# Window attention over row and column pairs: column heads staged in 128-channel tiles, one output product a block, stores of two blocks, and nine tiles off ScalarE in nine column pairs

## The chip, the cores and the metric

One core of one Trainium2 chip. The time is the device time of one execution in microseconds (us); shown are the runs of the kernel before and one profiled execution. TensorE is PE in the profile, VectorE is DVE, ScalarE is ACT, GpSimd is POOL, and SyncE, which issues most DMAs, is SP.

## What is computed

A picture `x` of 224 x 224 tokens with 96 channels gets queries, keys and values by one product with `wqkv`. The first 48 channels attend within horizontal stripes of 8 rows, the other 48 within vertical stripes of 8 columns; each stripe has 1792 tokens. The two results are joined channel by channel and multiplied with `wo`.

```python
qkv = jnp.einsum('bhwc,cd->bhwd', x, wqkv)
q, k, v = (qkv[..., :C], qkv[..., C:2 * C], qkv[..., 2 * C:])
scale = C2 ** (-0.5)                      # C = 96, C2 = 48, sw = 8
qh = q[..., :C2].reshape(B * nh, sw * W, C2)          # 28 horizontal stripes
ah = _softmax(jnp.einsum('bqc,bkc->bqk', qh, kh) * scale, axis=-1)
oh = jnp.einsum('bqk,bkc->bqc', ah, vh).reshape(B, H, W, C2)
...                                                   # ov: the same for 28 vertical stripes
o = jnp.pad(oh, ((0, 0), (0, 0), (0, 0), (0, C2))) + jnp.pad(ov, ((0, 0), (0, 0), (0, 0), (C2, 0)))
return jnp.einsum("bhwc,cd->bhwd", o, wo)
```

All arrays are bfloat16. The inputs are small, so the softmax is taken without a maximum; a mean key is taken off every key instead.

## The kernel before

**Stages.** Two stripes are worked at a time: 14 stages over row pairs (`P` from 0 to 13), then 14 over column pairs (`P` from 14 to 27). Stripe `w` of the pair lies in partitions `64 * w` and up. A stage has four chunks of queries (512, 512, 512 and 256 columns) against 14 blocks of 128 keys; a tile is one key block (two, in the last chunk) against one chunk for both stripes, 128 x 1024 scores. That makes 49 tiles a stage.

**A tile on ScalarE (kind A).** PE writes the scores into one of two pairs of PSUM banks (L689, four quarter products), ScalarE writes the exponentials of all 1024 columns into a buffer `PT` (L859), and PE multiplies them with V (L715), adding into one of four other banks, the ring.

**A tile off ScalarE (kinds P and R).** The exponential is worked out from a polynomial and a square. PE writes the scores into two banks of the ring (L702). DVE makes `qb` from their low halves (L943). For kind P, GpSimd squares `qb` into `PT` (L959), applies a scale and offset (L960), and squares again (L956); for kind R, DVE does a second pass (L945) and GpSimd only the one square (L956). Then PE writes the scores a second time (L702 again), and DVE joins them with `PT` (L948). Either DVE pass can be one instruction over both banks or two over one each. `KINDS` gives the tiles off ScalarE by chunk and `KIND_OF` the choice for each stage: eight in stage 0, nine (five P, four R) in stages 1 to 13, eight (five P, three R) in the columns.

**Order.** The work of PE is written out by hand in `ORDER`, one letter a step: q is a tile for ScalarE, v its product with V, 1 and 3 the first pass of a tile off ScalarE (one bank at a time, or both at once), 2 and 4 its second pass, k a step of preparing the next stage (K, the mean key, Q, V), g a part of the output product, f a part of the last pair's output. The mode A (q, 1 to 4, f) and the mode B (v, k, g) use the array in different shapes. `Sched.commit` turns each step into instructions with waits on semaphores; while it walks the letters it keeps estimated times (`tm`, `D_*`, `XR1`, `TURN`) to decide the order on DVE, GpSimd and the queues. These figures never run on the chip; they only decide who stands in front of whom. Each engine works strictly in its own order.

**Heads.** After a chunk, DVE copies its sums out (`emit_ot`, L876). A DMA transpose on SP's queue (`turn_ot`, L423) turns them to tokens in partitions, and GpSimd multiplies with the reciprocals of the sums (`emit_norm`, L920). For a row pair the result is `ohn`, and `keep_oh` copies it by DMA into the place of all column pairs in `cat` (96 channels a token, row heads in the first 48). For a column pair it goes into the last 48 channels of `cat`. `turn_cat` (L445) then transposes this pair's 28 blocks of 128 tokens x 96 channels with a DMA, 128 x 128 at a time: 28 x 96 / 128 = 21 tiles, in two parts of 12 and 9. So the blocks don't begin at the start of a tile, but at one of four offsets.

**Output.** `out_fills` (L623) does five blocks a step. A block's 96 channels lie in one transposed tile or in two, so a block takes one product or two, each in halves of 64 tokens (L637), against six shifted copies of `wo` with zeros around (`wo6`). DVE copies the sums into `cat` (L642), and a store of each block, 128 tokens of 192 bytes, follows on SP's queue (`emit_evict`, L897). The last pair is different: its row-head half is multiplied early, and `fin_fills` (L585) adds the column half at the end, block by block (L602, L609, L614), with stores on SP's, ScalarE's and GpSimd's queues.

**Start.** The first row pair is loaded directly by four DMAs of 168 KB, two on SP's queue and two on ScalarE's, then `wqkv` on SP's (L315 to L320); PE transposes it (L737), with DVE and ScalarE copying out (L749, L753). GpSimd sets constants meanwhile (L300 to L362).

Of the kernel before, what the change touches and what calls it, by code (L numbers as in the profile page):

```python
# [5 lines left out]
BF16 = mybir.dt.bfloat16  # L6
FP16 = mybir.dt.float16
FP32 = mybir.dt.float32
# [12 lines left out]
KINDS = ["PPR PPR PP ", "PPR PRR PPR ", "PPR PPR PR "]  # L21
# [11 lines left out]
D_ST, D_SW, D_TAIL = 0.64, 1.3, 0.70  # L33
XR1, XR2, TURN = 19.5, 43.0, 4.5
D_H, D_F, D_SQ, D_AF = 0.604, 1.137, 1.9, 1.03
# [4 lines left out]
NTWICE = 11  # L40


KIND_OF = [0, 1, 1, 1, 1, 1, 1, 1, 1, 1, 1, 1, 1, 1, 2, 2, 2, 2, 2, 2, 2, 2, 2, 2, 2, 2, 2, 2]
ORDER = [
    "kkkqkq3qkq3qkkqkq1qkqq1q3qvkqv2qvkqv2qvqkkvqv1qkvqvkqvv2qvqv1qvvvqvkq2vqvkqkq1qkvvq2qvv2qvvq1vqkvqvvq1vqv2qvkvqvkvq",
    "1vqvvqvq2vvq3qvvvqvv3qqvqvvqkkkq2qvqvkvqv2qkvqv2qkvvvq1qvvvvqvqvv1qvvq2vq2qvkqvvq1vqvkq2vqv2qvvq1qvvqvkqvvkqkvqvkq2vvq2qvv3",
    "qvvqv1qvvq1vqvvqvvqv1qkq1qvvvqvq2qvkkqvqvk2qvvq3qvkqvkvq4qkqv1qvvq4qvkq2vqv1qvq4vqkq2vqv1qvvqvvqv2q1qvvqvkkqq1vkv",
    "qv2qvqv1qvvvqvvqv1qq1vvqvvqvvvq4qvkvq1vqvvqvq2vqv1qvv4qkqvv1qvqvkq2vqkvvq2vkqvkq3vqkqvvvqv1qvq4vqkq3vqkvq4vqvkvq4vqkvq2vk",
    "qvvq1vqvvvvqq2vvvqvvvq2vqvq14qvqkqv3qvkvqvvqvkqv1qkqvvq1vqvkq2vqvkq2qvvvq1qv1qkqvvvqkqvvkq2qvv3qkvqv3qvvqv4qvkqv4qkqvv1",
    "qvqvvvq2vqq1vvqvv1qvvqvqv2qq4vqvkq1vqvvvqvq1vqkvkqkvvq2kqv3qkvqv4qvvqkq1vqvvvqkqvv4qvqkv2qvvq2vqv1qvq4vqvvqkvkvq1qkvvq2v",  # L50
# [123 lines left out]
def bass_standalone__window_attn_cswin__vision_kernel(  # L174
# [28 lines left out]
    with es:  # L203
# [1153 lines left out]
```

## Time and profile before

| | us |
|---|---|
| runs of the kernel before (three) | 1061.93, 1062.24, 1062.27 |
| profiled execution, its own time | 1062.68 |
| span of that execution in the trace | 1060.9 |
| first exponential begins (L859) | 9.57 |
| GpSimd's first square begins (L959) | 12.81 |
| last exponential ends | 1055.98 |
| granted TensorE clock, mean | 0.999 |

In rows of costly groups stand the line, engine, operation and names, then the count, the busy time, the mean duration in ns, and the idle time of that engine just before these instructions with what ended it. A row of the windows has the stretch and its length, then the busy time of PE, PEld (weight loads), DVE, ACT and POOL with counts, the granted clock and the DMA share. A row of a timeline has the start, the length, the engine and line, and how many such instructions follow one another. Instructions of one engine can overlap, so a mean duration can be longer than the pace.

### The profile page before, as it was taken

Reading aid. Unit: us, or ns where it says so; the run is one execution under the profiler, and the core shown is the slowest. Engines: PE = TensorE matmul, PEld = TensorE weight load, DVE = VectorE, ACT = ScalarE, POOL = GpSimd, SP = SyncE. Lnnn points to the kernel's source line nnn. Section 1 sums busy time; section 2 is a strip of 40 time slices with the busy share of each in tenths; the row PEclk is TensorE's granted clock in tenths of the full one; section 3 lists DMA queues with packets and bytes.
Section 4 is the critical chain, followed back from the end, with each engine's and each line's share of the span. In section 5 each row is a group of like instructions: output and inputs, shape, how many; then the busy total and the mean of one; then the engine's idle time right before and its main releaser. Section 6 shows DMA issues by size and latency. Waiting matters only on the chain.

```text
span 1060.9 us, 33547 instructions
## 1 busy us (share of the span) xinstructions
PE 1033.4 (97%) x13812; PEld 393.5 (37%) x13812; DVE 998.2 (94%) x1720; ACT 1049.3 (99%) x1146; POOL 935.5 (88%) x617
## 2 busy tenths in 40 slices
PE   9999999999999999999999999999999999999998
PEld 4333333333333333333334433333343443344433
DVE  8999999999999999999999999999999999999988
ACT  8999999999999999999999999999999999999998
POOL 7999999999988989999999778888888878979784
PEclk9999999999999999999999999999999999999999
DMA  9987648754963874322115334423332342332342
GB/s 182 160 153 112 100 80 145 112 96 84 144 96 56 139 108 69 38 56 58 40 20 99 76 54 76 88 38 77 80 69 52 81 83 49 79 79 40 64 65 44
DMA packets 376217, 88.58 MB, mean 83 GB/s; under 512 B 366944, under 2 KB 373376, under 8 KB 376064
## 3 DMA queue, kind: packets, MB, share of 16 engines
q1 hardware_dynamic: 374816, 85.85, 46.8%
q8 instruction: 108, 1.77, 0.7%
q10 hardware_dynamic: 1120, 0.49, 0.2%
q14 instruction: 45, 0.37, 0.1%
q0 software_dynamic: 128, 0.10, 0.0%
HBM read 28.36 MB, written 28.21 MB: 53 GB/s over the span
## 4 chain that ended last, share of the span: by engine, by line
PE 54%; ACT 28%; DVE 7%; issue 6%; POOL 4%; DMA 0%; ACTq 0%; POOLq 0%; DVEq 0%
ACT PT L859 28%; PE ps L715 20%; PE ps L689 20%; PE ps L702 7%; PE ps L521 3%; DVE qb L943 2%; DVE PT L948 2%; PE ps L637 2%; POOL PT L959 2%; PE ps L566 1%; POOL PT L956 1%; POOL PT L960 1%; DVE PT L945 1%; DVE KT_sb L526 1%; POOL cat L920 0%
## 5 line engine op out<-in xcount | busy, mean ns | idle before, releaser
L859 ACT ACTIVATE PT<-ps 128x1024 bf16<-128x1024 f32 x1135 | 1044.8, 1087 | 2.8 <-PE ps L689 1.8
L689 PE MATMUL ps<-QT_sb,KT_sb 49*64 49x512 bf16 (+1 forms) x5368 | 465.3, 363 | 17.6 <-ACT PT L859 10.5
L956 POOL TENSOR_TENSOR PT<-PT 128x1024 f16<-128x1024 f16 x237 | 445.1, 1892 | 41.1 <-DVE PT L945 24.1
L715 PE MATMUL ps<-PT,V_sb 128*49 128x512 bf16 (+1 forms) x3136 | 464.7, 362 | 0.3
L948 DVE SCALAR_TENSOR_TENSOR PT<-ps,PT 128x512 uint16<-128x512 f32 (+1 forms) x398 | 302.0, 787 | 20.8 <-PE ps L702 13.5
L943 DVE TENSOR_SCALAR qb<-ps 128x512 f16<-128x512 int16 (+1 forms) x404 | 302.3, 778 | 20.3 <-PE ps L702 15.8
L959 POOL TENSOR_TENSOR PT<-qb 128x1024 f16<-128x1024 f16 x141 | 266.1, 1892 | 54.8 <-DVE qb L943 24.9
L689 PEld LDWEIGHTS ps<-QT_sb,KT_sb 49*64 49x64 bf16 x5368 | 136.4, 103 | 305.8 <-ACT PT L859 280.9
L715 PEld LDWEIGHTS ps<-PT,V_sb 128*49 128x49 bf16 x3136 | 134.8, 103 | 211.1 <-issue 181.4
L702 PE MATMUL ps<-QT_sb,KT_sb 53*64 53x512 bf16 (+1 forms) x1896 | 189.4, 389 | 4.0 <-DVE PT L948 0.7
L960 POOL TENSOR_SCALAR PT<-PT 128x1024 f16<-128x1024 f16 x141 | 147.1, 1043 | 12.0
L945 DVE SCALAR_TENSOR_TENSOR PT<-ps,qb 128x512 f16<-128x512 int16 (+1 forms) x166 | 122.5, 766 | 0.5
L702 PEld LDWEIGHTS ps<-QT_sb,KT_sb 53*64 53x64 bf16 (+1 forms) x1896 | 53.8, 104 | 71.2 <-DVE PT L948 21.7
L876 DVE CAST OT_sb<-ps 113x512 bf16<-113x512 f32 x112 | 69.1, 617 | 3.0 <-PE ps L715 2.7
L535 DVE CAST QT_sb<-ps 128x512 bf16<-128x512 f32 (+1 forms) x111 | 67.2, 616 | 2.5 <-PE ps L521 1.7
L526 DVE TENSOR_SCALAR_CACHE_REDUCE KT_sb<-ps 128x512 bf16<-128x512 f32 x108 | 65.4, 616 | 1.3 <-PE ps L521 0.6
L642 DVE CAST cat<-ps 128x480 bf16<-128x480 f32 x84 | 51.5, 617 | 5.1 <-PE ps L637 4.5
L573 DVE CAST V_sb<-ps 128x480 bf16<-128x480 f32 (+1 forms) x84 | 51.7, 620 | 1.5 <-PE ps L566 1.2
L521 PE MATMUL ps<-xT_sb,w_sb 97*64 97x512 bf16 (+1 forms) x224 | 40.7, 364 | 0.0
L521 PE MATMUL ps<-xT_sb,wq_sb 97*64 97x512 bf16 x224 | 40.5, 366 | 0.1
L637 PE MATMUL ps<-wo,oc_all 128*64 128x96 bf16 x1176 | 39.9, 208 | 0.0
L566 PEld LDWEIGHTS ps<-w_sb,xT_sb 96*64 96x64 bf16 x1568 | 33.1, 112 | 17.7 <-issue 7.4
(64 smaller groups left out, 254.7 us busy)
## 6 DMA issues: line engine op xcount, KB each, us to landing
xT_sb<-xt_dram SPq DMA_DIRECT2D x28, 336.0 KB, 4.0
out_dram<-cat SPq DMA_DIRECT2D x382, 24.0 KB, 1.9
xp_dram<-in_x_dram SPq DMA_DIRECT2D x26, 336.0 KB
oc_all<-xp_dram SPq DMA_DIRECT2D x26, 336.0 KB, 4.4
xt_dram<-xT_sb SPq DMA_DIRECT2D x26, 336.0 KB, 6.4
cat<-ohn SPq DMA_DIRECT2D x52, 84.0 KB, 3.2
xt_dram<-xT_sb SPq DMA_DIRECT2D x4, 168.0 KB, 5.3
OT_tr<-OT_sb SPq DMA_TRANSPOSE x40, 3.4
```

Of the source, the lines that this page charges most:

```text
L521: ins = e.matmul(bk[64 * w:64 * w + 64, 0:qs], lhsT=lw, rhs=xT_sb[b][0:C + 1, w, q0:q0 + qs], start=True, stop=True)
L526: return e.tensor_scalar(KT_sb[b][:, q0:q0 + qs], bk[:, 0:qs], alpha, None, ALU.mult, ALU.add, accum_out=ksum[b][:, c:c + 1])
L689: ins = e.matmul(bank(SETS[s] + w)[64 * kh:64 * kh + 64, i * t["qs"]:(i + 1) * t["qs"]], lhsT=KT_sb[b][64 * w:64 * w + CA, kt * 128 + 64 * ...
L702: ins = e.matmul(bank(bp[w])[64 * kh:64 * kh + 64, 0:512], lhsT=KT_sb[b][64 * w:64 * w + nr, kt * 128 + 64 * kh:kt * 128 + 64 * kh + 64], ...
L715: ins = e.matmul(bank(pb)[64 * w:64 * w + CA, 0:t["qs"]], lhsT=V_sb[b][:, w, kt, :], rhs=PT[slot][:, ca:ca + t["qs"]], start=st and i == 0 ...
L859: S.commit("act", 0.0, D_ACT, None, lambda e, s=s, slot=slot: e.activation(PT[slot][:], ps[:, 512 * SETS[s]:512 * SETS[s] + 1024], ACTF.Ex ...
L943: fn, reads, writes = lambda e: e.tensor_scalar(q, l, m, a, ALU.mult, ALU.add), bk, qk
L945: fn, reads, writes = lambda e: e.scalar_tensor_tensor(y.bitcast(FP16), l, -RA * 2.0 ** 16, q, ALU.add, ALU.mult), bk + qk, ptk
L948: fn, reads, writes = lambda e: e.scalar_tensor_tensor(y.bitcast(U16), f, 128.0, y.bitcast(FP16), ALU.mult, ALU.add), bk + ptk, ptk
L956: square = ("pool", D_SQ, lambda e: e.tensor_tensor(y, y, y, ALU.mult), yk + ["pser"], yk)
L959: return [("pool", D_SQ, lambda e: e.tensor_tensor(y, q, q, ALU.mult), qk, yk), ("pool", D_AF, lambda e: e.tensor_scalar(y, y, -(QS * (RB ...
L960: ("pool", D_AF, lambda e: e.tensor_scalar(y, y, -(QS * (RB + RA) / 2) ** 2, 1.0, ALU.add, ALU.mult), yk + ["pser"], yk),
```

## The change

- **Nine pairs.** `KINDS` gets a fourth entry with nine tiles off ScalarE (six P, three R). Stages 15, 16, 17, 19, 20, 21, 23, 24 and 25 use it; 14, 18, 22, 26 and 27 stay at eight.
- **Order.** 23 of the 28 lines of `ORDER` are new; the lines of the middle of the row half are kept. A capital K or G stands for two steps of the same sort that fill two neighbouring banks and are copied out by one DVE instruction (`do_fill2`, `emit_both`); there is one of each.
- **Staging.** `cat` is replaced by `oh_all` (the kept row heads of all pairs, 48 channels a token), two staging tiles `stg` (one pair each, 28 blocks of 128 channels, the last 32 of them zero), and three output tiles `og`. For each column pair a new DMA on SP's queue, `rows_in`, copies the row heads from `oh_all` into `stg`, in runs of 96 bytes; `emit_norm` writes the column heads beside them. For the last pair and the first, both copies stand at the changeover, ahead of the last pair's transposes.
- **Products.** `turn_cat` transposes 28 tiles of 128 x 128 instead of 21. A block is one tile, so it takes one product (in two halves) against one copy of `wo`.
- **Stores.** A half of the array now takes a whole key block, and the products take every second token of it, so that two neighbouring tokens end up in one partition. A store covers two blocks: 128 partitions of 384 bytes. A column pair has 14 stores, and so has the last.
- **Start.** The first half of the load is cut in four DMAs of 84 KB, the second in two of 168 KB; `wqkv` goes over GpSimd's queue. The memsets of `stg` (448 and 1792 words of 32 bits a partition) join GpSimd's constants at the start, and the ones for `cat` and `wo6` (672 and 288 words) go from the later ones.

```diff
-KINDS = ["PPR PPR PP ", "PPR PRR PPR ", "PPR PPR PR "]
+KINDS = ["PPR PPR PP ", "PPR PRR PPR ", "PPR PPR PR ", "PPR PPR PPR "]
...
-KIND_OF = [0, 1, 1, 1, 1, 1, 1, 1, 1, 1, 1, 1, 1, 1, 2, 2, 2, 2, 2, 2, 2, 2, 2, 2, 2, 2, 2, 2]
+KIND_OF = [0, 1, 1, 1, 1, 1, 1, 1, 1, 1, 1, 1, 1, 1, 2, 3, 3, 3, 2, 3, 3, 3, 2, 3, 3, 3, 2, 2]
...
-    "v1qvvqvvqvvq2gqvvvq1vqgvqgvq2vqvvq2vvq3qvqgvq2vqvq1vqfvvqvvfqvfqvfqvv2qgqvvq1q2qvgqvvq1gqvqvvqv2qvvfqvfqvvfqvfq2vqvvqvqvvffqfvvvvfvff",
+    "q2qvvv1qvvq2vqv2qvvvq1qvvvqvvq1qvvq4vgqvvq1vqv2qvvq3vqgvvqvvqvq2vfqvvfqvvfqv1qvvq4vqgvq4vqgvqvv1qfqvvvqvvfqv4qvqg2qvfqfvvfqvvqvgqvvgvffvvvvfvff",
...
-        cat = sb("cat", [128, NPH, NPH, 2, C], BF16)
+        oh_all = sb("oh_all", [128, NPH, NPH, 2, C2], BF16)
+        stg = [sb(f"stg{i}", [128, NKT, 2, 128], BF16) for i in range(2)]
+        og = [sb(f"og{i}", [128, NKT // 2, 2, 2, C], BF16) for i in range(3)]
...
+        for h2, q in ((0, "sp"), (1, "actq")):
+            for w in range(2):
+                dma(q, [], [("x", w, 0, h2)], x0_sb[:, w, h2 * FQ:(h2 + 1) * FQ, :],
+                    x_lead[w][:, h2 * FQ * C:(h2 + 1) * FQ * C], f"x{w}0{h2}", land=3.1 + 0.4 * w + 0.2 * h2)
+        for w in range(2):
+            dma("sp", [], [("x", w, 1, 0), ("x", w, 1, 1)], x0_sb[:, w, FTH:2 * FTH, :],
+                x_lead[w][:, FTH * C:2 * FTH * C], f"x{w}10", land=4.7 + 0.3 * w)
...
+        dma("gq", [], ["wst"], wst[:, :], wqkv, "w0", land=4.6)
...
-            pool_now([("cat", NPH - 1)], lambda e: e.memset(cat[:, NPH - 1, :, :, C2:C].rearrange("p m w c -> p (m w) c").bitcast(FP32), 0.0), 0.7)
-            pool_now(["wo6z"], lambda e: e.memset(wo6[:].rearrange("p v c -> p (v c)").bitcast(FP32), 0.0), 0.3)
+        pool_now([("stgz", 0)], lambda e: e.memset(stg[0][:, :, :, C:].rearrange("p m w c -> p (m w) c").bitcast(FP32), 0.0), 0.5)
+        pool_now([("stgz", 1)], lambda e: e.memset(stg[1][:, :, :, :].rearrange("p m w c -> p (m w c)").bitcast(FP32), 0.0), 1.8)
...
+        def rows_in(P):
+            b = P % 2
+            dma("sp", ["oh", ("stgz", b)], [("sr", b)], stg[b][:, :, :, 0:C2].rearrange("p m w c -> p (m w) c"),
+                oh_all[:, P - NPH, :, :, :].rearrange("p m w c -> p (m w) c"), f"ri{b}")
...
-            turn(f"oc{b}{z}", ["oh", ("cat", a), ("ov", a, z)], [("ocT", b, z), ("catd", a, z)] + x_old,
-                 oc_T[b][:, k0 * 2 * C // 128:k1 * 2 * C // 128, :], flat[:, k0 * 2 * C:k1 * 2 * C])
+            turn(f"oc{b}{z}", [("sr", b), ("sc", b, z), ("stgz", b)], [("ocT", b, z)] + x_old,
+                 oc_T[b][:, 2 * k0:2 * k1, :], stg[b][:, k0:k1, :, :].rearrange("p m w c -> p (m w c)"))
...
-        dst_all = out[0].rearrange("(kt hh) (j dw) c -> j kt hh dw c", hh=16, dw=8)
+        dst_all = out[0].rearrange("(kp hh) (j dw) c -> j kp hh (dw c)", hh=32, dw=8)
...
-                        q, r = divmod(3 * (k0 + s), 4)
-                        use = {0: ((0, 0),), 3: ((0, 1), (1, 2)), 2: ((0, 3), (1, 4)), 1: ((0, 5),)}[r]
-                        for i, (dq_, v) in enumerate(use):
-                            for h in range(2):
-                                ins = e.matmul(bk[64 * h:64 * h + 64, s * C:(s + 1) * C], lhsT=oc_T[b][:, q + dq_, 64 * h:64 * h + 64],
-                                               rhs=wo6[:, v, :], start=i == 0, stop=i == len(use) - 1)
+                        m, u = divmod(k0 + s, 2)
+                        for h in range(2):
+                            ins = e.matmul(bk[64 * h:64 * h + 64, s * C:(s + 1) * C],
+                                           lhsT=oc_T[b][0:C, 4 * (m // 2) + 2 * h + m % 2, :].rearrange("c (t u) -> c u t", u=2)[:, u, :],
+                                           rhs=wo6[0:C, :], start=True, stop=True)
...
-                st = [] if last else [(P, (k0 + s) % 2, (k0 + s) // 2) for s in range(n)]
+                st = [] if last else [(P, m % 2, m // 2, sorted({("og", b, 2 * m // FS * FS), ("og", b, k0)})) for m in range(k0 // 2, (k0 + n) // 2)]
...
-                    dma(q, [key], [], dst_all[2 * (P - NPH) + w, kt], cat[:, P - NPH, kt, w, :], "op" if q == "gq" else f"out{P % 2}")
+                    P, w, kp, keys = item
+                    dma(q, keys, [], dst_all[2 * (P - NPH) + w, kp],
+                        og[2 if P == NP - 1 else P % 2][:, kp, w, :, :].rearrange("p s c -> p (s c)"), "op" if q == "gq" else f"out{P % 2}")
...
                 if ph_of(P):
-                    tm["sp"] = max(tm["sp"], st) + 1.5
+                    tm["sp"] = max(tm["sp"], st) + (2.2 if P > NPH else 1.5)
+                    if P > NPH:
+                        rows_in(P)
```

In `fin_fills` the last pair's products take every second token in the same way, and a store follows when both of its blocks are added. `emit_both` joins the two scale or copy instructions of K, Q, V or G into one over two banks.

202 lines of the change are left out of this document (137 added, 65 removed).

## The prediction

> **What bounds the kernel now.** I read the page first (busy shares, costliest groups), then the timeline of ScalarE alone, then who waited for whom, and last the busy time of each engine by stretch, cut at the first exponential of each stage (a stage is one row or column pair).
>
> ```profile
> span 1060.9 us, 33547 instructions
> PE 1033.4 (97%) x13812; PEld 393.5 (37%) x13812; DVE 998.2 (94%) x1720; ACT 1049.3 (99%) x1146; POOL 935.5 (88%) x617
> L859 ACT ACTIVATE PT<-ps 128x1024 bf16<-128x1024 f32 x1135 | 1044.8, 1087 | 2.8 <-PE ps L689 1.8
> L637 PE MATMUL ps<-wo,oc_all 128*64 128x96 bf16 x1176 | 39.9, 208 | 0.0
> ```
>
> ScalarE does 1135 exponentials and stands idle for 2.8 us before all of them together. PE also shows 97%, but its ends are modelled and its instructions overlap (the Trainium skill, "Trainium Kernel Development and Optimization", Performance Expectations, calls matmul busy time a bad measure of closeness to the limit; the weight loads' 37% here agrees that the array isn't full). The pace of ScalarE comes from its timeline, where two unbroken runs stand:
>
> ```profile
> 161.73 403.08 ACT L859 ACTIVATE PT<-ps 128x1024 bf16<-128x1024 f32 x438 [0.26 <-DVE PT L945]
> 565.17 375.61 ACT L859 ACTIVATE PT<-ps 128x1024 bf16<-128x1024 f32 x408 [0.36 <-PE ps L689]
> ```
>
> One lasts 1.087 us, but they overlap: (375.61 - 1.09) / 407 = 0.920 us from start to start in the columns, and (403.08 - 1.09) / 437 = 0.920 in the rows. So a tile on ScalarE costs 0.920 us, with either nine or eight of a stage's 49 tiles kept off it.
>
> ```profile
> PEld ps L689 <- ACT PT L859: 280.9, 803, 0.8
> ```
>
> This row of the waits says who is early: before 803 of the 1135 tiles PE had the next scores' weights ready and waited for ScalarE. In the other 332 (29%) PE came late or just in time.
>
> The windows give the room of the other engines. Columns: length, then busy us of PE, PEld, DVE, ACT, POOL. First the row stages 1 to 13, the changeover stage 14, column stages 15 to 25, 26 and 27:
>
> ```profile
> 47.80:526.70 478.90, 465.84 (x5828) 167.43 (x5824) 461.10 (x774) 478.34 (x522) 446.02 (x293) 1.00 0.58 94
> 526.70:565.20 38.50, 37.78 (x481) 13.61 (x480) 36.41 (x64) 38.02 (x43) 37.56 (x25) 1.00 0.26 52
> 565.20:980.70 415.50, 409.87 (x5854) 163.77 (x5850) 389.04 (x643) 415.15 (x452) 355.28 (x221) 1.00 0.35 70
> 980.70:1018.20 37.50, 37.46 (x552) 14.87 (x550) 33.97 (x61) 37.50 (x43) 28.99 (x19) 1.00 0.42 61
> 1018.20:1056.00 37.80, 36.71 (x514) 14.65 (x510) 33.47 (x78) 37.77 (x42) 25.87 (x19) 1.00 0.27 52
> ```
>
> The rows, at nine tiles off ScalarE, run with DVE 461.1 / 478.9 = 96.3% and POOL 93.1% busy. The column half (the last four rows, 529.3 us) has DVE 492.9 (93.1%) and POOL 447.7 (84.6%). So the bound is ScalarE, with a second limit close behind it.
>
> **The change part by part. Nine tiles leave ScalarE:** 9 x 0.920 = **-8.3 us**. Each becomes a P tile: two passes of scores on PE, two DVE passes, three POOL operations.
>
> ```profile
> L956 POOL TENSOR_TENSOR PT<-PT 128x1024 f16<-128x1024 f16 x237 | 445.1, 1892 | 41.1 <-DVE PT L945 24.1
> L948 DVE SCALAR_TENSOR_TENSOR PT<-ps,PT 128x512 uint16<-128x512 f32 (+1 forms) x398 | 302.0, 787 | 20.8 <-PE ps L702 13.5
> L943 DVE TENSOR_SCALAR qb<-ps 128x512 f16<-128x512 int16 (+1 forms) x404 | 302.3, 778 | 20.3 <-PE ps L702 15.8
> L959 POOL TENSOR_TENSOR PT<-qb 128x1024 f16<-128x1024 f16 x141 | 266.1, 1892 | 54.8 <-DVE qb L943 24.9
> L960 POOL TENSOR_SCALAR PT<-PT 128x1024 f16<-128x1024 f16 x141 | 147.1, 1043 | 12.0
> ```
>
> DVE: 237 tiles are off ScalarE now (the count of L956), so one costs (302.3 + 302.0) / 237 = 2.55 us; nine cost 22.9. POOL: 1.892 + 1.043 + 1.892 = 4.83 us; nine cost 43.4. On a column half of 529.3 - 8.3 = 521.0 us, DVE would be 515.8 (99.0%) and POOL 491.1 (94.3%). It fits, barely. The DVE figure is an upper one, since an instruction that another follows at once overlaps it (the pair at 1047.07 in the last fence takes 1.29 us, not 2 x 0.69). Within a stage it won't fit evenly: stages 15 to 25 hold all nine, and 389.0 + 22.9 = 411.9 exceeds 415.5 - 8.3 = 407.2. But the new order lets the off-ScalarE work lag. Counting its digits between the q's, stages 15 to 25 get only 10 of the 18 new passes (176 become 186), the others go to 14, 26 and 27 (two, two and four more), where DVE and POOL have room.
>
> What such density costs in pace I take from stages. The two with most and with least POOL work, of each half (changeover and last stage left out):
>
> ```profile
> 195.60:232.60 37.00, 36.13 (x456) 12.77 (x454) 36.02 (x62) 36.98 (x41) 36.19 (x24) 1.00 0.71 111
> 306.20:342.80 36.60, 35.53 (x446) 12.75 (x444) 35.58 (x65) 36.60 (x42) 30.57 (x20) 1.00 0.56 95
> 379.70:416.20 36.50, 35.74 (x446) 12.96 (x442) 34.85 (x59) 36.50 (x41) 31.64 (x20) 1.00 0.64 97
> 416.20:453.10 36.90, 35.66 (x452) 12.54 (x448) 35.84 (x63) 36.90 (x41) 36.08 (x23) 1.00 0.52 75
> 715.90:753.60 37.70, 36.69 (x524) 14.52 (x518) 34.01 (x56) 37.70 (x43) 28.65 (x19) 1.00 0.34 66
> 753.60:791.50 37.90, 37.26 (x534) 14.78 (x530) 35.23 (x59) 37.88 (x43) 35.02 (x23) 1.00 0.37 74
> 904.70:942.80 38.10, 37.80 (x548) 15.34 (x546) 35.64 (x60) 37.90 (x43) 34.78 (x23) 1.00 0.34 69
> 980.70:1018.20 37.50, 37.46 (x552) 14.87 (x550) 33.97 (x61) 37.50 (x43) 28.99 (x19) 1.00 0.42 61
> ```
>
> The four heavy ones sum to 149.9 us, the four light ones (same tile counts) to 148.3: 0.40 us a stage, for 5.56 us more of POOL work (142.07 against 119.85) and 1.08 of DVE's (142.73 against 138.41). By POOL: 43.4 x 0.40 / 5.56 = **+3.1 us** of lost pace. By DVE the slope is steeper: 22.9 x 0.40 / 1.08 = 8.5, the upper end; the lower is 0, as the rows keep 0.920 us at a like density. I take 3.1, since GpSimd work is what differs most between those stages.
>
> **PE.** The output stage's products fall from 1176 (84 a column pair) to 784 (56), all with 96 rows of contraction. They go in pairs, one for each half of the array:
>
> ```profile
> 759.80 0.34 PE L637 MATMUL ps<-wo,oc_all 128*64 128x96 bf16 x8
> ```
>
> (0.34 - 0.21) / 3 = 0.043 us a pair, so 196 pairs fewer save 8.4 us of PE. The nine second passes add 9 x 0.217 (the pace of a tile's products, from the last fence) = 2.0. Net -6.4, which counts only where PE is the late one: at most 29% of it, 1.9; at least 0. I take half, **-0.9**.
>
> The weights of these products, and of the last pair's, are now every second token of a tile. No row shows a strided load: the bounds are nothing (as the loads of L637 now) and, from its weight-load row below, one bare load a pair.
>
> ```profile
> L637 PEld LDWEIGHTS ps<-wo,oc_all 128*64 128x64 bf16 x1176 | 31.9, 110 | 16.0 <-issue 6.2 <-DVE PT L948 1.7 <-DVE qb L943 1.1
> ```
>
> That would be 392 x 0.110 = 43.1 us in place of 392 x 0.043 = 16.9: 26.2 more. I take nothing, since only the step of the address changes. The Trainium skill ("SBUF — State Buffer", Door 1: The DMA port swizzle) says that accesses within one 16-byte line run at full rate, up to a step of 8 bf16; step 2 is free by that. No run here shows it yet.
>
> **SP's queue and the transposes.**
>
> ```profile
> L287 SPq DMA_DIRECT2D out_dram<-cat x382: 538/598/1897, 594.5 to 1058.0; - x191
> L287 SPq DMA_DIRECT2D xt_dram<-xT_sb x30: 313/1700/4047, 17.0 to 420.6; - x30
> L414 SPq DMA_TRANSPOSE oc_all<-cat x28: 1282/1434/2536, 560.3 to 1031.3; - x28
> ```
>
> A column pair has 14 stores instead of 28: -14 x 0.598 = -8.4 us of issue. Added: one copy of the kept heads into the staging tile (nearest: the 1.70 us of the equally fine xt copies; 0.31 to 4.05), and a third more transposed tiles, 2 x 1.434 / 3 = 1.0. The queue gets some 5.7 us lighter a stage. The copy sits ahead of the pair's transposes and loads, nothing else waits behind it; the products that use them come later, and L637 shows idle 0.0 before it. So 0 for both signs; at the changeover two such copies stand in the queue, but the new order places its first product 17 exponentials into stage 15 (9 now). The two joined evictions (K, G) save under 0.1 us of DVE each: 0.
>
> **Lead.**
>
> ```profile
> 0.74 0.89 SPq L287 DMA_DIRECT2D cat<-in_x_dram  x2
> 3.99 3.22 PE L737 MATMUL ps<-ident,cat 112*96 112x112 bf16 x32 [0.33 <-DMA cat<-in_x_dram]
> 12.81 1.89 POOL L959 TENSOR_TENSOR PT<-qb 128x1024 f16<-128x1024 f16 x1 [3.29 <-DVE qb L943]
> L359 POOL MEMSET cat<- 128x672 f32 x1 | 0.7, 664 | 0.1
> ```
>
> PE's first transposes wait for a load of 168 KB; now they wait for half of that. Issue and start don't shrink, so between 0 and a quarter of the 3.2 us, 0.8; the later halves are issued third and fourth, 0.45 us apart, which caps it near 0.4. I take **-0.3**. POOL's two new memsets (448 and 1792 words: 0.664 x 2240 / 672 = 2.2 us) and one DMA issue (about 0.55) lie in its 3.29 us of idle before the first square; without that cover they would be at most 2.8 us of GpSimd, early in stage 0.
>
> **Tail.** After its last q the old order has 5 v and 4 f, the new one 8 v, 5 f and a g.
>
> ```profile
> 1054.68 1.06 PE L715 MATMUL ps<-PT,V_sb 128*49 128x256 bf16 x16
> 1056.02 0.13 PEld L715 LDWEIGHTS ps<-PT,V_sb 128*49 128x49 bf16 x4 [0.22 <-ACT PT L859]
> 1047.07 1.29 DVE L948 SCALAR_TENSOR_TENSOR PT<-ps,PT 128x512 uint16<-128x512 f32 x2 [0.17 <-PE ps L702]
> ```
>
> Four v's: (1.06 - 0.41) / 3 = 0.217 each. Three more are 0.65, a short g 0.13, one change of mode each way and an f about 0.3: 1.1, less the 0.22 that PE waits there now, and fewer stores queue at the end. 0 to +1.1; I take **+0.6**.
>
> Sum: -8.3 + 3.1 - 0.9 - 0.3 + 0.6 = **-5.8 us**. The profiled execution took 1062.68 us (1060.9 of span, 1.8 around it), which gives 1056.9; the median of the runs, 1062.24, lies 0.44 below it, so I predict **1056.4**. The ends of all terms give -11.1 and +1.3, so 1051.1 to 1063.5.
>
> **Rivals.**
>
> *ScalarE alone decides* (chance 0.24). The pace stays 0.920, as in the rows at nine tiles, so the 3.1 falls away: 1053.3. For it: the rows' 96.3% and 93.1%. Against it: 0.40 us between heavy and light stages.
>
> *DVE becomes the bound* (0.11, slower). DVE hands the four banks that PE fills back only as fast as it is free; if it can't be busier than the rows' 96.3%, the column half takes 515.8 / 0.963 = 535.6 us, 6.3 more than now: 1062.24 + 6.3 + 0.3 = 1068.8. It decides against the change if the share that can be reached is under 515.8 / 529.3 = 97.4%; the busiest shown stage, at 195.6, has 36.02 / 37.0 = 97.4%. Against it: the overlap of dense instructions, and the lag into stages 26 and 27.
>
> *The gain is given back* (0.09). The slope by DVE, 8.5 in place of 3.1: 1061.8.
>
> *Strided weights are slow* (0.05). PE gains 26.2 us of work; 29% of 26.2 is 7.6 on the path in place of part of the saving: 1056.4 + 7.6 = 1064.0, no change or a little slower.
>
> **How the numbers follow.** The forecast (1054 to 1059) has 0.51. Differences under 0.2%, 2.1 us, are no change here. Faster than 1060.1: the forecast, the first rival and part of the third, 0.80. Within: the rest of it and most of the fourth, 0.08. Slower: 0.12. The range 1051.5 to 1062.0 leaves out the slower cases and a gain beyond the sum of the best ends.
>
> **What would show it.** 1126 exponentials at 0.92 to 0.93 us in the columns confirm the first two terms; over 0.935 disproves the sum. DVE's share in the column half: at or under 97% with ScalarE waiting for PE and PE for DVE, the slower rival. L637 x784 with pairs at 0.043 us clears the strided loads; 0.11 convicts them. The first exponential before 9.57 us shows the lead's term, the time from the last one's end to the end of the span (5 us now) the tail's. New idle of PE before L637, or of POOL before L920, would show that the staging copy is late, which I hold for free.

## The result and the profile after

The changed kernel takes **1071.51 us** (median of six runs, 1069.34 to 1077.61), beside 1062.26 for the kernel before in the same comparison (1061.93 to 1063.39): ratio 1.0091, 95% interval 1.0065 to 1.0117. It is slower by 0.9%, where 1056.4 was forecast. The profiled execution took 1072.49 us, 1070.7 of it span. In all that follows, a median counts every run, while a ratio leaves out a run that took over 1.5% longer than the fastest of its kernel.

From the page of the changed kernel: the span, the busy shares, three of the costliest groups and one row of the DMA issues. The line numbers have moved: the exponentials are L873 now (L859), the output products L650 (L637), `emit_norm` L972 (L920).

```profile
span 1070.7 us, 32750 instructions
PE 1029.8 (96%) x13456; PEld 387.1 (36%) x13456; DVE 1015.2 (95%) x1749; ACT 1043.0 (97%) x1137; POOL 982.6 (92%) x651
L873 ACT ACTIVATE PT<-ps 128x1024 bf16<-128x1024 f32 x1126 | 1038.4, 1081 | 17.2 <-PE ps L703 15.5
L972 POOL TENSOR_TENSOR stg<-OT_tr,rn 128x768 bf16<-128x768 bf16 (+1 forms) x26 | 34.1, 1312 | 11.7 <-DVE rn L957 9.6
L650 PE MATMUL ps<-wo,oc_all 96*64 96x96 bf16 x784 | 31.5, 209 | 10.0 <-DVE PT L997 9.1
stg<-oh_all SPq DMA_DIRECT2D x15, 336.0 KB, 6.2
```

Nine exponentials are gone, as meant, but ScalarE now stands idle for 17.2 us before them instead of 2.8. PE's products had no idle before them and now have 10.0, most of it behind DVE; GpSimd's normalization has 11.7, most of it behind the reciprocals. Those are the two signs that the prediction named for a late staging copy.

Cut at the first exponential of each stage, the spans of three profiled executions differ in one place above all (the last column is the best version, e14 below):

| part of the span, us | before | changed | e14_four_late |
|---|---|---|---|
| to the first exponential | 9.57 | 10.51 | 9.26 |
| stages 0 to 13 | 517.10 | 516.61 | 516.68 |
| stage 14 | 38.49 | 38.90 | 38.78 |
| **stage 15** | 37.68 | **48.27** | 36.97 |
| stages 16 to 27 | 453.12 | 449.80 | 447.59 |
| end of the last exponential to the end | 4.92 | 6.60 | 6.63 |

Stage 15, the first after the changeover, takes 10.6 us more although ScalarE has one tile fewer in it. Its row in the windows of the kernel before, then of the changed kernel (length, busy PE, PEld, DVE, ACT, POOL, granted clock, DMA share, GB/s):

```profile
565.20:602.90 37.70, 37.45 (x554) 15.65 (x552) 34.92 (x57) 37.70 (x42) 33.60 (x21) 1.00 0.35 71
```

```profile
566.00:614.30 48.30, 38.48 (x522) 14.94 (x521) 36.83 (x67) 37.13 (x42) 36.81 (x24) 0.89 0.72 89
```

All four engines do their usual work and all have some 10 us of idle: so nothing became too busy, something was waited for. The DMA share has doubled, and the clock is 0.89. ScalarE's timeline and DVE's waits (total, times, longest) in the changed kernel say where:

```profile
597.68 1.94 ACT L873 ACTIVATE PT<-ps 128x1024 bf16<-128x1024 f32 x2 [9.90 <-PE ps L703]
```

```profile
DVE rn L957 <- DMA OT_tr<-OT_sb: 11.3, 4, 9.3
DVE qb L995 <- PE ps L716: 8.8, 30, 0.8
```

A reciprocal (L957) waits for the DMA transpose that brings its sums: 11.3 us in four waits, 9.3 in one. In the kernel before, the same 40 reciprocals (L905) have no such wait. The chain of waits of the changed kernel, in order of time (start, length, what), shows what that transpose had in front of it:

```profile
562.42 2.92 DMA oh_all<-ohn
...
565.35 6.30 DMA stg<-oh_all
...
571.67 7.58 DMA oc_all<-stg
...
579.27 3.69 DMA oc_all<-stg
...
587.46 6.03 DMA OT_tr<-OT_sb
...
593.51 0.23 DVE rn L957
593.74 1.14 DVE qb L995 x2
594.88 0.61 DVE PT L997
...
595.53 0.61 PE ps L650 x10
```

SP's queue works strictly in order. The row heads of the last row pair land at 565.33, then both staging copies go out (the second lands after 9.5 us). The last pair's two transposes wait for the first copy to land and go one after the other, then come a third copy and the loads, and only at 587.46 the transpose of stage 14's own last heads. It lands at 593.49. In DVE's strict order its reciprocal stands in front of two first passes, which PE needs to go on. So DVE, then PE, then ScalarE stop. On SP's queue of the kernel before, the same transpose of stage 14's last heads went out 7.6 us after the row heads had landed, not 22.1:

```profile
560.29 4.99 SPq L414 DMA_TRANSPOSE oc_all<-cat  x2
...
567.87 1.24 SPq L414 DMA_TRANSPOSE OT_tr<-OT_sb  x1
```

The clock follows. Windows of the changed kernel over the stall:

```profile
585.00:590.00 5.00, 1.41 (x14) 0.35 (x12) 0.00 (x0) 2.78 (x4) 0.14 (x1) 1.00 1.09 163
590.00:595.00 5.00, 0.00 (x0) 0.00 (x0) 1.49 (x4) 0.00 (x0) 1.11 (x1) 0.52 1.15 168
595.00:600.00 5.00, 4.47 (x36) 1.41 (x36) 3.59 (x6) 1.94 (x2) 4.83 (x5) 0.50 0.42 79
600.00:605.00 5.00, 5.00 (x84) 1.98 (x81) 4.83 (x9) 4.55 (x6) 3.08 (x2) 0.96 0.28 52
```

PE does nothing from 586.4 to 595.5, the granted clock falls to a half, and stays there for five more us while PE works again.

### The profile page after: what moved, and what is told of

It is laid out like the page before. It is cut to its first block, busy times and chain, and to the rows that moved or that the text cites. A ratio compares the mean times of both kernels' runs of the same rounds, so it can differ in the third digit from the quotient of the medians.

```text
span 1070.7 us, 32750 instructions
## 1 busy us (share of the span) xinstructions
PE 1029.8 (96%) x13456; PEld 387.1 (36%) x13456; DVE 1015.2 (95%) x1749; ACT 1043.0 (97%) x1137; POOL 982.6 (92%) x651
## 4 chain that ended last, share of the span: by engine, by line
PE 47%; ACT 21%; DVE 15%; POOL 6%; issue 6%; DMA 4%; SPq 0%; ACTq 0%; POOLq 0%; DVEq 0%
ACT PT L873 21%; PE ps L729 17%; PE ps L703 17%; PE ps L716 7%; DVE PT L1000 5%; DVE qb L995 4%; POOL PT L1008 3%; PE ps L536 3%; DMA OT_tr<-OT_sb 2%; DVE PT L997 2%; POOL PT L1011 2%; PE ps L581 1%; PE ps L650 1%; DMA oc_all<-stg 1%; DVE OT_sb L890 1%
## 5 line engine op out<-in xcount | busy, mean ns | idle before, releaser
L873 ACT ACTIVATE PT<-ps 128x1024 bf16<-128x1024 f32 x1126 | 1038.4, 1081 | 17.2 <-PE ps L703 15.5
L1008 POOL TENSOR_TENSOR PT<-PT 128x1024 f16<-128x1024 f16 x246 | 461.7, 1893 | 22.0 <-DVE PT L997 10.8
L1000 DVE SCALAR_TENSOR_TENSOR PT<-ps,PT 128x512 uint16<-128x512 f32 (+1 forms) x409 | 312.8, 793 | 15.4 <-PE ps L716 7.2
L995 DVE TENSOR_SCALAR qb<-ps 128x512 f16<-128x512 int16 (+1 forms) x421 | 313.4, 776 | 13.8 <-PE ps L716 8.8
L1011 POOL TENSOR_TENSOR PT<-qb 128x1024 f16<-128x1024 f16 x150 | 283.1, 1892 | 30.7 <-DVE qb L995 14.4
L716 PE MATMUL ps<-QT_sb,KT_sb 50*64 50x512 bf16 (+1 forms) x1968 | 197.2, 391 | 7.1 <-DVE PT L1000 1.6
L716 PEld LDWEIGHTS ps<-QT_sb,KT_sb 50*64 50x64 bf16 (+1 forms) x1968 | 55.8, 103 | 81.6 <-DVE PT L1000 25.8
L656 DVE CAST og<-ps 128x480 bf16<-128x480 f32 x82 | 50.0, 614 | 1.5 <-PE ps L650 0.7
L972 POOL TENSOR_TENSOR stg<-OT_tr,rn 128x768 bf16<-128x768 bf16 (+1 forms) x26 | 34.1, 1312 | 11.7 <-DVE rn L957 9.6
L536 PE MATMUL ps<-xT_sb,w_sb 97*64 97x512 bf16 x224 | 42.0, 372 | 0.5 <-DVE qb L995 0.2
L536 PE MATMUL ps<-xT_sb,wq_sb 97*64 97x512 bf16 x224 | 41.2, 368 | 0.1
L650 PE MATMUL ps<-wo,oc_all 96*64 96x96 bf16 x784 | 31.5, 209 | 10.0 <-DVE PT L997 9.1
```

What stands on the lines that cost most here:

```text
L536: ins = e.matmul(bk[64 * w:64 * w + 64, 0:qs], lhsT=lw, rhs=xT_sb[b][0:C + 1, w, q0:q0 + qs], start=True, stop=True)
L716: ins = e.matmul(bank(bp[w])[64 * kh:64 * kh + 64, 0:512], lhsT=KT_sb[b][64 * w:64 * w + nr, kt * 128 + 64 * kh:kt * 128 + 64 * kh + 64], ...
L873: S.commit("act", 0.0, D_ACT, None, lambda e, s=s, slot=slot: e.activation(PT[slot][:], ps[:, 512 * SETS[s]:512 * SETS[s] + 1024], ACTF.Ex ...
L995: fn, reads, writes = lambda e: e.tensor_scalar(q, l, m, a, ALU.mult, ALU.add), bk, qk
L1000: fn, reads, writes = lambda e: e.scalar_tensor_tensor(y.bitcast(U16), f, 128.0, y.bitcast(FP16), ALU.mult, ALU.add), bk + ptk, ptk
L1008: square = ("pool", D_SQ, lambda e: e.tensor_tensor(y, y, y, ALU.mult), yk + ["pser"], yk)
```

## The experiments

The theory formed from this: **SP's queue is late at the changeover, and a reciprocal that was placed in DVE's order by too early an estimate turns the lateness into a stall.** Rivals: nine tiles are too dense for DVE and GpSimd (A); PE waits for the staged data itself (B); the copies cost by their use of the DMA engines, wherever they stand (C). All kernels compute the whole result. Lengths of the stages that matter, in us, from one profiled execution of each:

| stage | before | changed | e1 | e2 | e4 | e5 | e8 | e11 | e12 | e13 | e14 |
|---|---|---|---|---|---|---|---|---|---|---|---|
| 1 | 36.93 | 36.90 | 36.83 | 36.79 | **41.62** | **41.58** | 36.77 | 36.73 | 36.93 | 36.87 | 36.72 |
| 15 | 37.68 | **48.27** | 39.64 | 37.36 | 37.31 | **56.56** | 36.95 | **49.44** | 36.93 | 38.05 | 36.97 |
| 16 | 37.72 | 37.77 | 36.79 | 37.65 | 37.18 | 37.43 | **44.27** | 37.45 | 36.86 | 37.28 | 36.83 |
| 19 | 37.70 | 37.67 | 37.45 | 37.53 | 37.34 | 39.50 | 37.39 | 37.51 | 36.98 | 36.89 | 36.85 |
| 25 | 37.89 | 37.61 | 37.45 | 37.47 | 39.01 | 37.83 | 37.45 | 37.35 | **49.73** | **48.45** | 37.38 |

**e1_rn_place: only the reciprocal's place.**

```diff
-                    dq.append(dict(what="rn", ready=tm["sp"] + TURN, ...
+                    dq.append(dict(what="rn", ready=tm["sp"] + TURN + (14.0 if (P, c) == (NPH, 3) else 0.0), ...
```

> The changed kernel with one edit: the planner's due time for the reciprocal of the second part of stage 14 is 14 us later, so DVE's strict order has it behind some 25 more instructions; DMAs, tiles and PE's order are the same. Theory (SP's queue is late at the changeover, the reciprocal stands too early in DVE's order and blocks DVE, then PE, then ScalarE): ScalarE's 9.9 us of idle in stage 15 falls under 1.5 us and the time from 1071.5 to 1061-1063. Rival A (nine tiles make DVE and GpSimd too dense in stage 15): DVE's work is the same, the stall stays, 1069-1073. Rival B (PE waits for the staged data itself, through the output products): the stall moves to PE's output products, 1066-1073.

Measured: 1062.63 us (1059.8 to 1063.4), ratio to before 0.9992 (0.9983 to 1.0002): the time of before. The data come as late as they did, and 8.6 of stage 15's 10.6 us are gone; ScalarE's longest idle there is 1.46 us. Rival A falls. Of rival B there is a remainder; PE's waits in stage 15 of this kernel, and its window:

```profile
PE ps L650 <- DMA oc_all<-stg: 1.6, 2, 1.4
```

```profile
566.40:606.00 39.60, 37.93 (x522) 14.97 (x522) 36.52 (x67) 37.22 (x42) 37.54 (x24) 0.96 0.93 112
```

**e2_rows_early: the copies' place.**

```diff
+                        if P == NPH - 2:
+                            rows_in(NP - 1, 0, NPH - 1)
+                            rows_in(NPH, 0, NPH - 1)
...
-                            rows_in(NP - 1)
-                            rows_in(NPH)
+                            rows_in(NP - 1, NPH - 1, NPH)
+                            rows_in(NPH, NPH - 1, NPH)
```

> The changed kernel with the row heads of pairs 0 to 12 copied into the two staging tiles one stage earlier, right after they are kept; only the last row pair's heads are copied at the changeover (two copies of a fourteenth each). DVE's order is the same. Theory (late SP queue): the data of the second part of stage 14 land some 10 to 13 us earlier than 593.5, at 581 to 584, the wait of the reciprocal goes from 9.3 us to under 2, the time to 1061-1064. Rival A (density of stage 15): no change, 1069-1073. Rival C (the copies' cost is their use of the DMA engines beside the transposes, wherever they stand): the stall moves one stage ahead and the time stays above 1067.

The DMA issues of this kernel, and DVE's timeline at the reciprocal:

```profile
stg<-oh_all SPq DMA_DIRECT2D x13, 336.0 KB, 6.0
stg<-oh_all SPq DMA_DIRECT2D x2, 312.0 KB, 7.5
stg<-oh_all SPq DMA_DIRECT2D x2, 24.0 KB, 2.0
```

```profile
582.75 0.23 DVE L957 RECIPROCAL rn<-OT_tr 128x12 f32<-128x12 bf16 x1 [0.24 <-DMA OT_tr<-OT_sb]
```

With 2.0 us for each small copy at the changeover, the reciprocal runs at 582.75 after 0.24 us of waiting. This execution was 1.7 us ahead at the start of stage 15 (564.2 against 566.0), so the data came 9 us earlier; 10 to 13 were expected. Stage 15 takes 37.36 us, and stage 14, where the copies stand now, no longer than in the changed kernel (38.84), so rival C falls. But of ten runs six took 1059.3 to 1061.7 us and three 1066.6 to 1067.7, these with a mean clock of 0.991 instead of 0.999; one took 4489 us, which nothing here explains. The median is 1061.5, the ratio 1.0003 (0.9983 to 1.0024).

**e4_order_alone: the kernel before, with the new kinds and order, and nothing else.**

```diff
-KINDS = ["PPR PPR PP ", "PPR PRR PPR ", "PPR PPR PR "]
+KINDS = ["PPR PPR PP ", "PPR PRR PPR ", "PPR PPR PR ", "PPR PPR PPR "]
...
-KIND_OF = [0, 1, 1, 1, 1, 1, 1, 1, 1, 1, 1, 1, 1, 1, 2, 2, 2, 2, 2, 2, 2, 2, 2, 2, 2, 2, 2, 2]
+KIND_OF = [0, 1, 1, 1, 1, 1, 1, 1, 1, 1, 1, 1, 1, 1, 2, 3, 3, 3, 2, 3, 3, 3, 2, 3, 3, 3, 2, 2]
```

(and the new `ORDER`, with kk for K and gg for G)

> The kernel before with the new kinds, the new order and nothing else: nine pairs have nine tiles off ScalarE; heads, products, stores and start as before, so SP's queue has no staging copies. Theory: no stall in stage 15; nine tiles 8.3 us off ScalarE less about 4 of lost pace, and about 1 more in the tail: 1057-1061. Rival A (density): stage 15 still takes about 10 us more than 37.7, 1066-1072.

The total is 1071.6 us (ratio 1.0081, 1.0066 to 1.0096), out of the theory's range and as rival A had it, but not for its reason: stage 15 takes 37.31 us, and the 40 reciprocals, here L905, wait for no transpose (the list after "until" is empty):

```profile
L905 DVE RECIPROCAL rn<-OT_tr x40: 217/244/320, 85.9 to 1037.2; 128x28 f32<-128x28 bf16 x14, 128x16 f32<-128x16 bf16 x13, 128x12 f32<-128x12 bf16 x13
its engine sat idle before it (us, times) until:
who waited for it (us, times):
...
```

So the same order with the same tiles, without the staging copies, has no stall at the changeover. Its loss is in stage 1 (+4.7), in stages 25 to 27 (117.4 against 113.2) and at the end (7.9 us after the last exponential): this order was written for the new start, products and stores, which is probably why. Stage 1 shows a half clock after a short lack of work:

```profile
60.00:65.00 5.00, 3.65 (x36) 1.11 (x38) 2.95 (x6) 4.38 (x5) 5.00 (x4) 0.90 1.20 161
65.00:70.00 5.00, 5.00 (x34) 0.91 (x26) 3.39 (x4) 3.31 (x4) 4.83 (x4) 0.50 1.26 181
```

**e5_staging_alone: the changed kernel with the kinds and the order of before.**

> The changed kernel with the kinds and the order of before: staging, single products, stores of two blocks and the new start, but eight tiles off ScalarE in every column pair. Theory: SP's chain at the changeover is as long as in the changed kernel, and the old order has its first output product earlier in stage 15, so DVE or PE waits there 9 to 14 us: 1070-1077. Rival A (density): nothing in stage 15, 1060-1063, as the staging is free.

1091.2 us (1080.9 to 1105.8; ratio 1.0234, 1.0182 to 1.0286), worse than expected. Stage 15 takes 56.6 us at a mean clock of 0.70, and DVE's waits there are led by the same wait:

```profile
DVE rn L957 <- DMA OT_tr<-OT_sb: 7.9, 2, 4.7
```

So the stall comes with the staging under the old order too, with eight tiles as with nine. It isn't a clean count of it: these two waits explain 7.9 of the 18.9 us that stage 15 gains, the clock stays at 0.50 from 585 to past 610, and the new products, stores and start are in this kernel as well. After its last exponential this kernel needs 5.1 us, like before: the longer end belongs to the new order.

**e8_both: e2 and the reciprocal of stage 14 due 5 us later.**

> The kernel with the row heads copied early (e2_rows_early), and the reciprocal of the second part of stage 14 due 5 us later in the planner. Theory (a late landing in front of a reciprocal that blocks DVE is all that stage 15 lost): with both, the data are there well before the reciprocal, no run shows a stall in stage 15, all runs lie within 1058-1063 and the runs at 1066-1068 of e2_rows_early, with a mean clock of 0.991, are gone. Rival: those runs have a stall elsewhere, and about a third of the runs stay at 1066-1068.

Nine runs took 1058.8 to 1061.1 us, the profiled one 1065.3 with a clock of 0.991, and one 1169.9 with a clock of 0.73, which I can't explain; the median is 1060.35, the ratio 0.9972 (0.9962 to 0.9982). So the rival was right in part. The profiled run has the clock of e2's three at 1067 and is probably of their kind, though none of those was kept as a trace: stage 15 is clean, stage 16 takes 44.3 us. PE's timeline and the windows there:

```profile
616.03 0.41 PE L716 MATMUL ps<-QT_sb,KT_sb 53*64 53x512 bf16 x4 [0.76 <-DVE og L656]
...
618.35 0.49 PE L716 MATMUL ps<-QT_sb,KT_sb 50*64 50x512 bf16 x4 [0.34 <-DVE PT L1000]
```

```profile
614.00:616.00 2.00, 1.27 (x14) 0.33 (x10) 0.96 (x4) 2.00 (x3) 2.00 (x2) 1.00 0.25 58
616.00:618.00 2.00, 1.97 (x36) 0.78 (x36) 2.00 (x3) 1.60 (x3) 2.00 (x2) 1.00 0.28 74
618.00:622.00 4.00, 3.66 (x32) 0.92 (x30) 2.55 (x5) 2.69 (x3) 3.83 (x4) 0.57 0.38 74
622.00:626.00 4.00, 4.00 (x36) 1.19 (x34) 3.38 (x6) 3.06 (x3) 3.65 (x3) 0.50 0.32 67
630.00:634.00 4.00, 4.00 (x28) 0.71 (x20) 2.85 (x5) 2.94 (x4) 1.86 (x2) 0.50 0.02 4
```

```profile
615.24 0.23 DVE L957 RECIPROCAL rn<-OT_tr 128x12 f32<-128x12 bf16 x1 [1.04 <-DMA OT_tr<-OT_sb]
```

DVE waits 1.04 us for stage 15's last heads, again transposed behind a staging copy and two loads; PE loses 0.76 and 0.34 us, and then runs some 17 us at half clock. In e2's profiled execution DVE waited 0.79 us at the same place, PE lost 0.49 and 0.34 us, and the clock stayed at 1.00.

**e9_more_r and e10_more_p: what sets the pace of nine tiles.** On e2, one kind in each of the nine column pairs: `"PPR PRR PPR "` (e9), `"PPP PPR PPR "` (e10) in place of `"PPR PPR PPR "`.

> e2_rows_early with kind R in place of kind P for one of the nine tiles of the nine column pairs: GpSimd has 2.94 us less a stage, DVE some 0.75 us more, PE and ScalarE the same. Theory 1 (the lost pace, 0.41 us in a nine-tile stage, is GpSimd's density; my slope was 0.40 us for 5.56 us of it): 0.21 us less in each of the nine stages, 1.9 in all, 1058-1059. Theory 2 (DVE's density, slope 0.40 us for 1.08): 0.28 us more in each, 2.5 in all, 1063. Theory 3 (PE's order sets it): within 0.7 us of e2_rows_early's runs without a stall.

> e2_rows_early with kind P in place of kind R for one of the nine tiles of the nine column pairs (seven P, two R): GpSimd 2.94 us more a stage, DVE some 0.75 less. Theory 1 (GpSimd's density): the nine stages 1.9 us longer in all. Theory 2 (DVE's density): 2.5 us shorter in all. Theory 3 (PE's order): no change in them beyond 0.7 us.

1098.3 us (ratio 1.0334, 1.0286 to 1.0382) and 1134.7 (two runs; 1.0678, 1.0605 to 1.0750), stages 16 to 25 together 413.0 and 435.2 us against e2's 373.5. No theory had that. In e10 DVE waits 32.6 us in 13 waits for output products of PE; in e9 ScalarE waits 35.6 us in 55 short ones. PE's order stayed as written for other kinds, so that engines miss each other, and clock is lost as well (0.969 and 0.964). That this is why they are so slow is argued, not shown. They don't tell GpSimd's density from DVE's; that stays open.

**e11_old_lead: e2 with the start of before** (two loads of 168 KB on each of two queues, `wqkv` on SP's).

> e2_rows_early with the loads of the start as before: four DMAs of 168 KB, and wqkv on SP's queue. My prediction's term: the first exponential 0.3 us later than with the new start, at the same granted clock. Theory now: the time of the first exponential (9.57 before, 10.51 changed, 8.62 in e2_rows_early) follows the moment at which the clock is granted in full, which differs from one execution to the next whatever the loads; so no change in the median beyond 1 us.

1070.1 us (ratio 1.0065, 1.0043 to 1.0086), and not because of a later start: the first exponential is at 8.79. The loss is in stage 15, 49.4 us long, at the same reciprocal (L952 here):

```profile
586.70 0.23 DVE L952 RECIPROCAL rn<-OT_tr 128x12 f32<-128x12 bf16 x1 [4.41 <-DMA OT_tr<-OT_sb]
```

It doesn't stand earlier than in e2: the traces have the same instructions on DVE in the same order, and on SP's queue too after the start. Its data come later, at 586.70 instead of 582.75, though stage 15 begins at 564.1 and 564.2. The last kept row heads land 1.4 us later than in e2, the last pair's two transposes take 1.1 us more and its own transpose 1.4. Why these DMAs are slower, and whether they are in the other three runs, stays open. So the run says little of the start, and much of how narrow the place of that reciprocal is: e2's order has hardly any slack there (a wait of 0.24 us), and 4 us of lateness make 12 us of stall.

**e12_all_late and e13_rn_all: all reciprocals of second parts due later.** e2, or the changed kernel, with 5 (14) us more for stage 14 and 3 us for every later column pair.

> e2_rows_early with the reciprocal of the second part due later for every column pair: 5 us for stage 14, 3 us for the others. Theory (a reciprocal that waits for transposed data holds DVE, PE runs dry, and the granted clock may halve): the waits of the 40 reciprocals, 11.3 us in the changed kernel, 2.2 in e2_rows_early and 0 before, go under 0.5; no run shows a mean clock under 0.997; all runs at 1058-1061.5; stages 16, 19 and 21 get shorter. Rival (the runs at 1066 come from elsewhere): some runs stay at 1065-1068.

> The changed kernel with both copies at the changeover, as it is, and the reciprocal of the second part due later for every column pair: 14 us for stage 14, 3 us for the others. Theory: only DVE's order is changed, and the data stay late; what is left of the stall is PE's own wait for the transposed tiles in stage 15 (2 us in e1_rn_place). 1060-1062.5. Rival: as e1_rn_place or slower, 1062.6 and more, since the later waits are no part of the loss.

The waits of the reciprocals fall to 0.4 and 1.5 us, and in e12 stages 16 and 19 take 36.9 and 37.0 us as expected (21 doesn't: 37.3 against 37.1). Yet both kernels are slower: 1076.5 us (ratio 1.0135, 1.0117 to 1.0154) and 1074.7 (1.0106, 1.0075 to 1.0137), by a new wait in stage 25. PE's and ScalarE's rows in e12:

```profile
PE ps L650 <- DMA oc_all<-stg: 8.6, 1, 8.6
```

```profile
980.01 1.02 ACT L873 ACTIVATE PT<-ps 128x1024 bf16<-128x1024 f32 x1 [8.91 <-PE ps L703]
```

There the reciprocal had never waited. In e12 it runs 4.6 us later in the stage than in e2 (21.9 us after the stage's first exponential, not 17.2), GpSimd takes other tiles first and normalizes 16.7 us later (36.4 instead of 19.7), the transpose goes out behind that, and PE's products wait for it: rival B's wait, made by hand.

**e14_four_late: later only where it waited.**

```diff
+... + {14: 5.0, 15: 3.0, 18: 3.0, 20: 3.0}.get(P, 0.0) * (c == 3), ...
```

> e2_rows_early with the reciprocal of the second part due later only in the four stages where it waited in the changed kernel: 5 us for 14, 3 us for 15, 18 and 20. Theory (a reciprocal too early holds DVE; too late, as in stage 25 of e12_all_late, PE waits for the transposed tiles): the 40 reciprocals wait under 0.5 us in all, stages 16 and 19 take 36.9 and 37.0 us as in e12_all_late, stage 25 stays at 37.5, the mean clock is 0.997 or more in every run, and the time is 1057.5-1061, under the kernel before in every run. Rival (the slow runs of e2_rows_early come from elsewhere): some runs at 1065-1068.

**1058.65 us** (five runs, 1057.71 to 1059.05, clock 0.999 in all; ratio 0.9961, 0.9947 to 0.9974), 0.4% faster than the kernel before and as expected. From its page and its windows of stages 15 and 16:

```profile
L873 ACT ACTIVATE PT<-ps 128x1024 bf16<-128x1024 f32 x1126 | 1037.5, 1079 | 3.7 <-PE ps L703 2.6
```

```profile
564.70:601.70 37.00, 36.62 (x522) 14.66 (x520) 36.50 (x67) 36.95 (x42) 35.80 (x24) 1.00 0.63 100
601.70:638.50 36.80, 36.27 (x504) 14.42 (x500) 35.94 (x63) 36.79 (x41) 33.98 (x22) 1.00 0.51 89
601.70:1049.30 447.60, 439.31 (x6012) 171.51 (x6010) 433.80 (x745) 446.52 (x485) 414.45 (x262) 1.00 0.50 83
```

ScalarE's idle before its exponentials is 3.7 us instead of 17.2, stage 16 takes 36.83 us instead of 37.77, stage 25 stays. No reciprocal waits. No run is at 1067, but five are few: with e2's share, three of nine, none in five would come about one time in eight.

## Why the prediction was wrong

**The step that failed** is the one on SP's queue: "The copy sits ahead of the pair's transposes and loads, nothing else waits behind it ... So 0 for both signs". Two things were wrong in it.

First, the copy was priced by the time that its issue holds the queue (1.70 us, from the `xt` copies), and the wait for its landing was left out. The issue is even cheaper, 0.63 us in the median. But the transposes behind the copy need its data, so the queue stands until it has landed. The page of the kernel before had the time to landing for the same `xt` copies, 336 KB each; the changed kernel's staging copies are close to it, 6.2 us in the median (the row of the DMA issues above), and the second of two in a row takes 9.5:

```profile
xt_dram<-xT_sb SPq DMA_DIRECT2D x26, 336.0 KB, 6.4
```

```profile
L292 SPq DMA_DIRECT2D stg<-oh_all x15: 604/632/2536, 565.4 to 1027.8; - x15
```

Second, the list of who is behind the copy left out the transposes of the heads (`turn_ot`), whose reciprocals stand in DVE's order; I looked at the output products alone, and they were indeed late by only 1.6 us (e1). The planner had the same gap. Its term for the changeover went from `3.5 + 5.3` to `3.5 + 8.5`, so 3.2 us more, where the transpose of stage 14's last heads really goes out 14.5 us later after the row heads' landing (22.1 against 7.6). What the step cost: stage 15's 10.6 us. e1 (place of the wait), e2 (place of the copies) and e4 (no copies) each take away most or all of it.

**Nine tiles, -8.3**: right. Nine exponentials fewer, and with the stall gone (e14) stages 15 and 16 run at 0.921 to 0.924 us a tile. By the prediction's own sign, 0.92 to 0.93 over the 565 exponentials of the columns, e14 confirms it (0.926), while the changed kernel with its stall is at 0.950.

**Lost pace, +3.1**: about right in size, wrong in cause. Stages 16 to 27 lost 449.80 - (453.12 - 8 x 0.920) = 4.0 us. In e14, without the reciprocals' waits, it is 1.8. From e2 to e14, which differ in the reciprocals' places alone, these stages lose 2.0 us (449.5 to 447.6), so about 2 of the 4.0 came from those waits: SP's queue again, not GpSimd's density. What the 1.8 are is open (e9, e10).

**PE's relief, -0.9**: e4 and e14 run the same order with the old and the new products; over stages 16 to 24 e14 is 336.2 - 334.1 = 2.1 us shorter. Stores, staging and start differ between them too, so the term itself isn't measured.

**Strided weights, 0**: right. From the groups of the changed kernel, and from PE's timeline at full clock:

```profile
L650 PEld LDWEIGHTS ps<-wo,oc_all 96*64 96x64 bf16 x784 | 24.6, 110 | 24.4 <-DVE PT L997 10.7 <-issue 6.3 <-DMA oc_all<-stg 0.9
```

```profile
1062.19 0.38 PE L650 MATMUL ps<-wo,oc_all 96*64 96x96 bf16 x10
```

A load takes 110 ns as before, and five pairs go at (0.38 - 0.21) / 4 = 0.043 us each. This agrees with the Trainium skill, "SBUF — State Buffer", Door 1: The DMA port swizzle, by which steps within a 16-byte line run at full rate.

**Lead, -0.3**: not seen. PE's first transposes do begin earlier, at 3.3 us with the new start and at 3.9 to 4.2 with the old one, but that doesn't reach the first exponential. It began at 8.62 to 10.77 us in ten executions with the new start and at 8.79 to 10.33 in three with the old one. The difference goes with the length of PE's products: two products of L536 took 0.64 us at the changed kernel's start and 0.41 at e2's:

```profile
7.14 0.64 PE L536 MATMUL ps<-xT_sb,wq_sb 97*64 97x512 bf16 x2
```

```profile
6.22 0.41 PE L536 MATMUL ps<-xT_sb,wq_sb 97*64 97x512 bf16 x2
```

The Trainium skill ("TensorE: Matmul & The Clock Gate", Part 1) explains such differences by an activity window that runs free of the kernel's start; the spread here agrees with it. 0.64 us is also what products of 512 columns take in e8 while the granted clock is 0.50 (0.41 at 1.00). But the clock column of the windows reads 1.00 at both starts, so a half clock there is inferred from the lengths alone. Where these products take 0.41, the first exponential begins at 8.62 to 9.26 (new start) and 8.79 (old), where they take 0.64 at 9.96 to 10.77 and 10.33. So neither group shows a gain, and one of 0.3 can't be told from so few.

**Tail, +0.6**: mis-sized, 1.7 in the changed kernel, above its upper bound of 1.1. e5, with the new stores and the old order, needs 5.08 us, 0.16 more than before: it is the order. The 1.1 counted PE's extra work; the additions and stores behind it, which PE's lag pushes back, were left out, and they are probably the rest.

**The rivals.** DVE as the bound would have needed a share that can't exceed 96.3%; in e14's stages 16 to 27 it is 433.8 / 447.6 = 96.9%, in stage 15 even 36.5 / 37.0 = 98.6%, and no stall. So the slower outcome came by another mechanism than that rival's. The sign that was named for it, a share under 97% with ScalarE waiting for PE and PE for DVE, was there all the same (94.7% in the columns of the changed kernel): a stall of DVE looks like that too, whatever DVE waits for. Without the stall the sum was not far off: e14 is 4.1 us faster than before, 5.8 were forecast. (The prediction's lower end, -11.1, should be -10.6 by its own terms, -8.3 - 1.9 - 0.4. Nothing hangs on it.)

## What to carry to other kernels

A step that is moved or added on an in-order queue delays everything issued behind it there: list all of it, with the consumer of each and what stands behind that consumer on its own engine, not only the step's own reader. Price the step by its landing, not by its issue, when something behind it on the queue needs its data. An instruction that waits for a DMA in an in-order engine has a window: too early it blocks the engine (stage 15: 10.6 us), too late and the work behind its result is late in turn (stage 25: 12 us); the planner's estimate of the landing has to be measured again whenever the queue changes, and needs room, since the landing varies (e2 and e11: 4 us at the same order). Where PE is nearly full, a wait of 1 us may cost over 6 (e8's stage 16: 44.27 us against 37.65 in e2), since the clock can follow.

## What the runs showed of the hardware

- A staging copy from SBUF to SBUF, 336 KB in runs of 96 bytes, takes 6.2 us to land, and two together 6.3 and 9.5; its issue holds SP's queue for 0.63 us in the median. In the changed kernel a transpose of 16 tiles issued while such a copy is under way took 7.58 us and the next, of 12 tiles with none beside it, 3.69; in e2, with no large copy beside them, the two took 8.1 us together instead of 11.3.
- The granted clock fell to a half not only after a long pause: in e8 after 0.76 and 0.34 us of idle within some four, in e4's stage 1 after 1.3 us. In e8 it then stayed low for some 17 us while PE was busy all the time. e2's profiled execution kept its clock after 0.49 and 0.34 us at the same place. Between losing the clock and keeping it lay 0.27 us of idle in these two executions. That this is also why e2's runs fall into two groups 6 us apart (1059 to 1062 and 1067) is likely, not shown.
